# The first head of a hash-attention kernel: copies, sign products and the second head's transposes in another order

## The chip, the cores and the metric

The kernel runs on one core of a Trainium2 chip. The metric is the device time of one execution in microseconds (us), lower is better. TensorE (PE) multiplies matrices, VectorE (DVE), ScalarE (ACT) and GpSimd (POOL) work element by element, and SyncE (SP) issues most DMAs. PEld is PE's loading of weights, which overlaps its multiplications.

## The reference

Four batches of eight heads, 768 positions, head dimension 64. Each position of q and of k gets six sign bits from a projection (64x6); a query sees only keys with the same six bits. A feed-forward stage follows on all heads of a batch side by side.

```python
q_bits = (np.einsum('bhsd,dk->bhsk', q, proj) > 0)
k_bits = (np.einsum('bhsd,dk->bhsk', k, proj) > 0)
mask = q_bucket[:, :, :, None] == k_bucket[:, :, None, :]
scores = np.where(mask, scale * np.matmul(q, k.transpose(0, 1, 3, 2)), -1e9)
attn = softmax(scores)
x = np.matmul(attn, v)          # heads side by side: 512 columns
xk = mu_k * x + (1 - mu_k) * x_prev
xr = mu_r * x + (1 - mu_r) * x_prev
kk = np.maximum(xk @ w_k, 0)
out = sigmoid(xr @ w_r) * (kk * kk @ w_v)
```

## The kernel before

The work goes by pairs of heads: 16 pairs `n`, two heads `j` in each. One head's keys fall into six chunks of 128. A **slot** is one such chunk: two matmuls score all 768 queries against 128 keys (`score`, L451), ScalarE takes the exponential out of PSUM (L458), and two slots later PE multiplies it with the values (`pv`, L478). There are 192 slots. The loop over slots (L750) writes out the order of every engine's queue by hand: in slot G come the score of G, the value product of G-2, pieces of the feed-forward stage of the batch before (from pair 4 on), and what the table `first_block` names for the first slots. Nothing reorders it: an instruction that waits holds up all that stands behind it on its engine. A score tile has two buffers in PSUM, so the score of slot G waits for the exponential of G-2.

The mask is folded into the score. Each operand (`aq`, `ak`) has 70 rows: 64 of q or k, and six rows of +0.5 or -0.5 from the sign bits. A scaled exponential with a large negative bias then sends pairs with different bits to zero. So a score needs three things on each side: transposed q or k in fp32 (`tq`, `tk`), its cast to bf16 in the 64 rows, and the six sign rows.

- `turn` (L311) transposes one side of one head with three matmuls into a PSUM bank, copies the bank to `tq` or `tk`, and casts its two halves of 384 positions into the 64 rows (L336, L337). With `copy=True` ScalarE does the copy (L325) and the second half (L327) and GpSimd the first half (L326). Otherwise VectorE copies (L330 for q, L332 for k), and the casts are done by the engines in `casts`: `pool2` is GpSimd for both, the default is GpSimd and VectorE.
- `bits_direct` (L391) is used for the first pair: one fp32 matmul (two passes) with a projection that lies in `projd` for both halves, and then VectorE makes the sign rows, one instruction for each half of 384 positions (L397). `bits` (L403) does the same for a whole pair and moves the rows by DMA.
- `projd` is filled on VectorE (L695) from `projp`, which is loaded by a DMA on ScalarE's queue behind half of k (L73).
- The PSUM banks A, B, C and D hold one tile each; a new tile waits until the last one was read. Score tiles lie in a pool of their own with two buffers.
- Ahead of the first data, 22 matmuls on constants (L686) keep PE busy.

The order of PE before the loop is: idle matmuls, transposes of q and k of the first head, sign products of both (`bdq`, `bdk`), transposes of q and k of the second head. Then slot 0's score, slot 1's score, the second head's sign product of q, slot 2's score, its sign product of k, and slot 0's value product ahead of slot 3's score. VectorE's order is: copy of q, three copies of the projection, sign rows of q and k, copies of the second head, its sign rows.

Later, GpSimd also casts the values (`values`, L423), and moves the column for the shifted x (`turn_out`, L509), for which VectorE's difference `df` (L521) waits.

## Time and profile before

| what | value |
|---|---|
| three runs | 265.42, 265.53, 266.64 us; median 265.53 |
| profiled execution | 266.43 us, span 264.6 us |
| PE busy | 250.3 us, 95% of the span |
| ACT busy | 216.1 us, 82% |
| DVE busy | 180.0 us, 68% |
| POOL busy | 123.0 us, 46% |
| first transposes on PE | 4.09 us |
| first score on PE | 9.94 us |
| first exponential on ACT | 10.46 us |

The profiled execution is one of its own, outside of the three runs. The span is the time between the first and the last instruction; what lies around it is 1.8 us. The times below count from the span's start. In a timeline row the first number is the start, the second the busy time, "x3" the number of instructions that were merged, and the bracket says how long the engine was idle before and what ended that. In the chain of waits each row is a piece of the one path that leads to the last instruction. Matmuls overlap in the array, so rows of PE can begin before the one above has ended.

### The profile page before, as it was taken

Reading aid. Unit: us, or ns where it says so; the run is one execution under the profiler, and the core shown is the slowest. Engines: PE = TensorE matmul, PEld = TensorE weight load, DVE = VectorE, ACT = ScalarE, POOL = GpSimd, SP = SyncE. Lnnn points to the kernel's source line nnn. Section 1 sums busy time; section 2 is a strip of 40 time slices with the busy share of each in tenths; the row PEclk is TensorE's granted clock in tenths of the full one; section 3 lists DMA queues with packets and bytes.
Section 4 is the critical chain, followed back from the end, with each engine's and each line's share of the span. In section 5 each row is a group of like instructions: output and inputs, shape, how many; then the busy total and the mean of one; then the engine's idle time right before and its main releaser. Section 6 shows DMA issues by size and latency. Waiting matters only on the chain.

```text
span 264.6 us, 6633 instructions
## 1 busy us (share of the span) xinstructions
PE 250.3 (95%) x2441; PEld 151.5 (57%) x2441; DVE 180.0 (68%) x377; ACT 216.1 (82%) x320; POOL 123.0 (46%) x251
## 2 busy tenths in 40 slices
PE   6999999998999999999999999998999999999990
PEld 5566656665565656565665656564656665455450
DVE  2675588769897766759587876778595746776440
ACT  3388879988999998979999998988999988079600
POOL 3669798695766472804574474607492000000000
PEclk9999999999999999999999999999999999999998
DMA  7923695976959291949575483959310002220132
GB/s 217 372 69 54 217 256 92 161 175 119 235 142 185 65 222 34 236 150 247 152 174 109 113 173 88 208 191 237 95 57 8 1 2 83 79 79 0 39 142 73
DMA packets 26488, 35.41 MB, mean 134 GB/s; under 512 B 3064, under 2 KB 22992, under 8 KB 26448
## 3 DMA queue, kind: packets, MB, share of 16 engines
q1 hardware_dynamic: 23936, 31.89, 46.4%
q0 software_dynamic: 2144, 2.62, 6.7%
q8 instruction: 21, 0.34, 0.6%
q10 hardware_dynamic: 368, 0.39, 0.5%
q14 instruction: 19, 0.16, 0.2%
HBM read 30.68 MB, written 6.29 MB: 140 GB/s over the span
## 4 chain that ended last, share of the span: by engine, by line
PE 72%; ACT 9%; DVE 7%; POOL 4%; DMA 2%; issue 2%; SPq 0%; ACTq 0%; DVEq 0%; POOLq 0%
PE sc L451 17%; PE vp L553 15%; PE kp L553 14%; PE oo L478 9%; ACT pt L458 8%; PE rp L553 7%; PE bb L369 3%; PE oo L469 2%; PE ot L503 2%; PE bb L409 1%; DMA vf<-in_v_dram 1%; DMA qk<-in_q_dram 1%; PE bdq L395 1%; DVE ob L490 1%; DVE kr L578 1%
## 5 line engine op out<-in xcount | busy, mean ns | idle before, releaser
L458 ACT ACTIVATE pt<-sc,expb 128x768 bf16<-128x768 f32 x192 | 167.7, 910 | 20.6 <-PE sc L451 18.6
L451 PE MATMUL sc<-aq,ak 70*128 70x384 bf16 x384 | 93.7, 325 | 1.8 <-ACT pt L458 0.7
L478 PEld LDWEIGHTS <-pt 128*128 128x128 bf16 x1152 | 60.5, 97 | 26.5 <-issue 0.2
L478 PE MATMUL oo<-va,pt 128*128 128x65 bf16 x1152 | 66.3, 193 | 0.0
L553 PE MATMUL kp<-xk,wk_sb 128*128 128x384 bf16 x256 | 55.7, 325 | 2.8 <-DVE kr L578 1.1
L553 PE MATMUL vp<-wv_sb,k 128*128 128x512 bf16 (+1 forms) x200 | 51.9, 370 | 0.0
L451 PEld LDWEIGHTS <-ak 70*128 70x128 bf16 x384 | 34.8, 98 | 27.6 <-issue 6.7
L586 DVE TENSOR_TENSOR k<-kr 128x384 bf16<-128x384 bf16 x64 | 27.1, 438 | 6.4 <-ACT kr L576 5.9
L553 PEld LDWEIGHTS <-wk_sb 128*128 128x128 bf16 x256 | 21.7, 97 | 14.3 <-issue 3.8
L353 POOL CAST aq<-tq 64x768 bf16<-64x768 f32 x20 | 16.5, 824 | 26.8 <-PE sc L451 11.7
L553 PE MATMUL rp<-wr_sb,xr 128*128 128x512 bf16 x96 | 28.9, 379 | 0.1
L576 ACT ACTIVATE kr<-kp 128x384 bf16<-128x384 f32 x36 | 18.1, 503 | 8.0 <-PE kp L553 8.0
L553 PEld LDWEIGHTS <-k 128*128 128x128 bf16 x200 | 16.7, 97 | 12.9 <-issue 2.7
L509 POOL COPY xt<-xt 128x127 bf16<-128x127 bf16 x12 | 3.5, 294 | 42.6 <-DVE xt L504 42.5
L439 POOL TENSOR_TENSOR s<-vf 128x192 f32<-128x192 f32 x32 | 22.7, 708 | 0.0
L618 DVE SCALAR_TENSOR_TENSOR os<-th,vp 128x512 f32<-128x512 bf16 (+1 forms) x25 | 16.5, 661 | 7.3 <-PE vp L553 5.4
L489 DVE RECIPROCAL rc<-oo 128x6 f32<-128x6 f32 x32 | 6.1, 191 | 21.9 <-PE oo L478 21.8
L578 DVE TENSOR_SCALAR kr<-kp 128x384 bf16<-128x384 f32 x28 | 15.4, 551 | 7.3 <-PE kp L553 7.1
L504 DVE COPY xt<-ot 128x768 bf16<-128x768 bf16 x16 | 8.9, 556 | 14.8 <-PE ot L503 14.8
L490 DVE TENSOR_TENSOR ob<-oo,rc 128x384 bf16<-128x384 f32 x32 | 17.8, 557 | 1.1
L355 POOL TENSOR_SCALAR ak<-tk 64x768 bf16<-64x768 f32 x20 | 16.6, 832 | 2.8 <-DVE tk L343 1.3
L303 ACT ACTIVATE sq<-blk 128x768 bf16<-128x768 f32 x20 | 17.0, 852 | 0.0
(83 smaller groups left out, 305.5 us busy)
## 6 DMA issues: line engine op xcount, KB each, us to landing
blk<-in_q_dram SPq DMA_DIRECT2D x40, 176.0 KB
blk<-in_k_dram SPq DMA_DIRECT2D x40, 176.0 KB
vf<-in_v_dram SPq DMA_DIRECT2D x16, 384.0 KB
out_dram<-os SPq DMA_DIRECT2D x23, 256.0 KB
qk<-in_q_dram SPq DMA_DIRECT2D x5, 384.0 KB
qk<-in_k_dram SPq DMA_DIRECT2D x5, 384.0 KB
wk_sb<-in_moe_w_k_dram POOLq DMA_DIRECT2D x2, 512.0 KB, 5.5
wv_sb<-in_moe_w_v_dram POOLq DMA_DIRECT2D x2, 512.0 KB, 5.8
```

The source lines that it names most:

```text
L303: nc.scalar.activation(junk.rearrange("p (u d) -> p u d", u=NTOK), blks[n][:, i, :, 0:32], AF.Square, scale=1.5, accum_out=nrm[:, i, n : n ...
L353: eng.tensor_copy(dst, src)
L355: eng.tensor_scalar(out=dst, in0=src, scalar1=ALPHA, scalar2=1.0, op0=ALU.mult, op1=ALU.mult,)
L439: nc.gpsimd.tensor_add(s3, vf[:, 0 : 3 * D], vf[:, 3 * D : 6 * D])
L451: nc.tensor.matmul(sc[:, sp, 0:HALF], au["k", j][:, jc * P : (jc + 1) * P], au["q", j][:, sp * HALF : (sp + 1) * HALF], start=True, stop=True,
L458: nc.scalar.activation(pt.rearrange("p (s q) -> p s q", s=2), sc[:, :, 0:HALF], AF.Exp, bias=expb, scale=SCALE,)
L478: nc.tensor.matmul(oo[:, ic, :], pts[n, j, jc][:, ic * P : (ic + 1) * P], vas[n, j][:, jc, :], start=False, stop=(jc == NC_ - 1 and ic == ...
L490: nc.vector.tensor_tensor(out=obs[n][:, :, j * D : (j + 1) * D], in0=oo[:, :, 0:D], in1=rc.to_broadcast([P, NC_, D]), op=ALU.mult,)
L553: nc.tensor.matmul(box["t"], lhs(), rhs(), start=(i == 0), stop=(i == len(mms) - 1))
L576: nc.scalar.activation(kr, kp, AF.Relu, scale=HALFROOT)
L578: nc.vector.tensor_scalar(out=kr, in0=kp, scalar1=0.0, scalar2=HALFROOT, op0=ALU.max, op1=ALU.mult,)
L586: lambda: nc.vector.tensor_tensor(out=k2, in0=kr, in1=kr, op=ALU.mult),
```

## The change

Five things are done, all in the launch order; the result's arithmetic is the same.

1. Ahead of q's copy VectorE makes the two copies of the projection into `projd`; the third copy (`projp`, needed from the second pair on) comes after k's copy.
2. For the first head, q is copied with `copy=True` (ScalarE twice, GpSimd one cast) and k with `pool2` (VectorE's copy, GpSimd both casts); before, it was the other way round.
3. k's sign product is cut into two pieces, keys 0 to 127 in bank B and 128 to 383 in bank C. VectorE makes k's sign rows in four instructions (128, 256, 128 and 256 positions) instead of two of 384.
4. The second head's transposes move from ahead of slot 0's score to behind it (slot 0 of `first_block`). Idle matmuls: 26 instead of 22 ahead of the data, and eight new ones between k's sign product and slot 0's score, in one buffer of the score pool.
5. At slots 11 and 13 the second half of k's cast for pair 2 goes to VectorE instead of GpSimd.

```diff
-            def bits_direct(n, i, j, which):
+            def bits_direct(n, i, j, which, cuts=(0, HALF)):
 
                 side = "qk"[i]
-                bb = bank(which, [P, HALF], FP32, f"bd{side}{n}_{j}")
-                nc.tensor.matmul(bb, projd, t32s[n, side, j], start=True, stop=True)
+                parts = []
+                for w, lo, hi in zip(which, cuts, cuts[1:]):
+                    bb = bank(w, [P, hi - lo], FP32, f"bd{side}{n}_{j}_{lo}")
+                    nc.tensor.matmul(
+                        bb, projd, t32s[n, side, j][:, lo:hi], start=True, stop=True
+                    )
+                    parts.append((lo, hi, bb))
                 for e in range(2):
-                    nc.vector.tensor_scalar(
-                        out=augs[n % NSET][side, j][D:AUG, e * HALF : (e + 1) * HALF],
-                        in0=bb[D + 32 * e : D + 32 * e + NB, :],
-                        scalar1=0.0, scalar2=0.5, op0=ALU.is_gt, op1=ALU.subtract,
-                    )
+                    for lo, hi, bb in parts:
+                        nc.vector.tensor_scalar(
+                            out=augs[n % NSET][side, j][D:AUG, e * HALF + lo : e * HALF + hi],
+                            in0=bb[D + 32 * e : D + 32 * e + NB, :],
+                            scalar1=0.0, scalar2=0.5, op0=ALU.is_gt, op1=ALU.subtract,
+                        )
...
             idle = bank("A", [P, P], FP32, "idle")
-            for _ in range(22):
+            for _ in range(26):
                 nc.tensor.matmul(idle, epsm, epsm, start=True, stop=True)
             pool2 = (nc.gpsimd, nc.gpsimd)
-            turn(0, 0, 0, "B", pool2)
-            turn(0, 1, 0, "D", copy=True)
-            for dst in (
-                projd[0:D, D : D + NB],
-                projd[D:P, D + 32 : D + 32 + NB],
-                projp[D:P, NB : 2 * NB],
-            ):
+            for dst in (projd[0:D, D : D + NB], projd[D:P, D + 32 : D + 32 + NB]):
                 nc.vector.tensor_copy(dst, projp[0:D, 0:NB])
+            turn(0, 0, 0, "B", copy=True)
+            turn(0, 1, 0, "D", pool2)
+            nc.vector.tensor_copy(projp[D:P, NB : 2 * NB], projp[0:D, 0:NB])
             bits_direct(0, 0, 0, "A")
-            bits_direct(0, 1, 0, "C")
+
+            bits_direct(0, 1, 0, "BC", (0, P, HALF))
+            idle = scp.tile([P, P], FP32, name="idle1", tag="sc")
+            for _ in range(8):
+                nc.tensor.matmul(idle, epsm, epsm, start=True, stop=True)
...
             values(0, 0)
-            turn(0, 0, 1, "B", pool2)
-            turn(0, 1, 1, "D", pool2)
+
+            def turn_second():
+                turn(0, 0, 1, "B", pool2)
+                turn(0, 1, 1, "D", pool2)
+
...
             first_block = {
+                0: turn_second,
...
                 10: lambda: turn(2, 0, 0, "B", pool2),
-                11: lambda: turn(2, 1, 0, "D", pool2),
+                11: lambda: turn(2, 1, 0, "D"),
                 12: lambda: turn(2, 0, 1, "B", pool2),
-                13: lambda: turn(2, 1, 1, "D", pool2),
+                13: lambda: turn(2, 1, 1, "D"),
             }
```

## The prediction, made before the changed kernel ran

> **What bounds the kernel now.** I read the busy shares first, then the chain of waits over the first 14 us, then the timeline of that stretch engine by engine, because every edit but one lies before the fourth score.

> ```profile
> PE 250.3 (95%) x2441; PEld 151.5 (57%) x2441; DVE 180.0 (68%) x377; ACT 216.1 (82%) x320; POOL 123.0 (46%) x251
> ```

> TensorE is busy 95% of the span and its queue is fixed by hand, so an end that moves by some amount at the start moves the end of the kernel by as much, unless a wait further on swallows it. The chain of waits says what the start consists of:

> ```profile
> 4.09 0.89 PE tpq L318 x3
> ...
> 5.65 0.51 DVE projd L695
> ...
> 6.30 1.62 PE bdq L395 x2
> 7.92 1.29 PE bdk L395 x2
> ...
> 9.23 0.56 DVE ak L397
> ...
> 9.82 0.56 DVE ak L397
> ...
> 10.41 0.57 DVE tq L330
> ...
> 11.03 0.91 PE bdq L395 x2
> 11.94 0.33 PE sc L451 x2
> 12.27 0.65 PE bdk L395 x2
> ```

> Read it as: q's transposes, the projection's copy on VectorE, q's and k's sign products, k's sign rows in two halves, then the second head's copy of q (tq, 10.41), its sign product, and only then the third score. The first score ran at 9.94 and is not on this chain: the third score (11.78) is. From there on PE stands in its own queue: no row of PE up to the fourth score (13.10) has a wait, while ScalarE waits for it:

> ```profile
> 12.30 0.90 ACT L458 ACTIVATE pt<-sc,expb 128x768 bf16<-128x768 f32 x1 [0.15 <-PE sc L451]
> ```

> So the number to work out is when the third score issues.

> One later place also counts. Between 24 and 30 us the chain lies on GpSimd, whose casts end in xt, for which VectorE waits; behind that wait stand copies that PE needs at 33.17:

> ```profile
> 30.02 0.56 DVE L521 TENSOR_TENSOR df<-xt 128x768 bf16<-128x768 bf16 x1 [2.64 <-POOL xt L509]
> ...
> 33.17 0.55 PE L318 MATMUL tpk<-ident,qk 128*128 128x128 f32 x3 [0.43 <-DVE tk L332]
> ```

> **The change part by part, against the profiled execution (266.43 us, 264.6 of it span).**

> *Projection ahead of q, q copied by ScalarE.* Before, VectorE copies q (5.01 to 5.57) and then the projection; its second copy takes 0.50 us against 0.15 of the first, and bdq starts at 6.30, 0.14 after it. After, the projection's copies stand first on VectorE. Its DMA landed at 4.80 by the trace's landings, so two copies of 0.15 end near 5.2, at most 5.55 if the second again takes 0.50. ScalarE, idle there, copies q in 0.49 (row L325): 5.01 to 5.50. So bdq starts at 5.50+0.14 = 5.64, 0.66 earlier. ScalarE's second copy of q (0.49, to 6.0) frees bank B, and VectorE's copy of k (from 5.65, 0.55, to 6.20) feeds bdk, which stands behind bdq until 7.05: both hidden, with 0.8 us to spare. GpSimd's casts of k (two of 0.50) now end near 7.3, before a first score at 8.9 or later: hidden. Four more idle matmuls (22 take 2.53, one each 0.107) end near 3.85, before q's transposes at 4.09: nothing.

> *k's sign product in two pieces.* On PE it is the same 384 columns: bdq 5.64, bdk 7.05, free at 8.33. On VectorE, q's two rows start at 5.64+1.62+0.04 = 7.30 and take 1.13, to 8.43. Then four pieces of k (128, 256, 128, 256 columns) instead of two of 384. The trace has no 128-column piece; a copy of 8 columns takes 0.17 (L710) and one of 384 takes 0.56, so a piece lies between these. A straight line gives 0.29 and 0.42, which I take. First piece ends at 8.73, third at 9.46, fourth at 9.89.

> *Eight idle matmuls, then the first score.* They run 8.33 to 9.18 at 0.107 each, where the first piece alone would let the score go at 8.73+0.15 = 8.88: 0.3 us later, and on the path 0.06 (next step).

> *Second head's turns behind the first score.* This adds a wait. tpq of the second head takes bank B, so it waits for the third piece (9.46, so 9.60); the first score holds PE to 9.66. Behind it on PE's queue are tpk, the second score, and everything else. Three transposes issue 0.11 apart and are done 0.49 after the first: 10.15. VectorE copies q from 10.19 (before: 10.41) to 10.75, bdq follows at 10.80, the third score 0.75 later (11.03 to 11.78 in the rows): 11.55. Before: 11.78. **Gain 0.22 us**, a third of what bdq won: pieces, the wait for bank B and the later transposes give the rest back. The second score issues at 10.32 and its exp runs from 10.85 (before 11.26), so ScalarE only waits longer before the third.

> *Key casts of pair 2 half on VectorE.* GpSimd loses two casts of 0.50, so xt comes about 1.1 earlier; df, tq and aq then run early, but the reciprocal behind them (31.36) waits for head sums that PE ends near 31.13, so the rest of that queue comes only 0.19 earlier and PE's wait of 0.43 shrinks by that. VectorE gains two casts of 0.36 to 0.64 (rows L337), the first ahead of the next q copy (23.46, where it had 0.25 idle). That pushes the k copy that the sign products at 25.41 wait for by 0.11 to 0.39, of which they have about 0.1 to spare (it ends at 25.22); of the 0.01 to 0.29 left I take 0.13, nearer the short casts, since GpSimd has fewer left to collide with. Net gain 0.06.

> [...]

> **Sum:** 266.43 − 0.22 − 0.06 = 266.15 for a run like the profiled one. The runs' median is 265.53, 0.90 below it, so the same gain of 0.28 gives 265.25, put down as **265.2 us**.

> **The rivals.** They turn on PE's rate. The same pair of bdq matmuls takes 1.62 at 6.30 and 0.91 at 11.03, three transposes 0.87 at 4.09 and 0.49 at 9.54: until about 9.4, PE ran at half speed, though the granted clock reads 1.00.

> *Full speed comes earlier (faster).* With 26 idle matmuls PE's gap before the transposes shrinks from 0.51 to 0.25 and the one before bdq from 0.69 to 0.25. If that brings full speed before bdq, its 1.62 become about 0.95, and the third score wins 0.65 more; if before the transposes, another 0.3 at most, as the projection lands at 4.80. That is 264.3 to 264.6. Against: the times (265.42, 265.53, 266.64, and 266.43 profiled) fall in two groups 1 us apart, just the size of this step, so the median may hold it already, and then 265.2 stands. Chance 0.17. [...]

> *Full speed comes later (slower).* If PE's waits for VectorE put the change past the first scores, the work from 9.4 to 12 (2.32 us busy in that window) runs at half rate. It takes 2.3 longer, less some 0.6 that PE and ScalarE wait there anyway: 265.2 + 1.7 = 266.9. [...] Chance 0.05.

> *The pieces cost as much as halves.* If a piece takes 0.56 whatever its width, the third ends 0.68 later, and the third score comes 0.46 later than before: 265.9. [...] Chance 0.25. For it: VectorE's rows hardly shrink for few partitions (6 rows cost as much as 128). Against: 8 columns take 0.17. Should they take 0.17 each, PE's 9.66 still binds, so nothing is won.

> **How the numbers follow.** Forecast 0.53 (264.9 to 265.6), earlier full speed 0.17 (264.3 to 264.9), costly pieces 0.25 (265.6 to 266.2), later full speed 0.05. Leaving out the slow case and the ends of the others, the range is 264.5 to 266.2. Half a per cent, about what a measurement of this kernel can tell from no change, is 1.33 us: faster than 264.2 needs the earlier clock and every bound at its best (0.06); slower than 266.86 needs the later clock (0.05); within, 0.89.

> **What would show it.** bdq starting near 5.65 and tq on ScalarE at 5.01; VectorE's first piece near 0.29 us; idle matmuls ending after the first piece; the second head's tpq waiting for VectorE or following the first score at once, near 9.6; the third score near 11.55; the wait of df on xt cut to about 1.5 us and PE's 0.43 at tpk halved. I am wrong if the pair of bdq takes 0.9 rather than 1.6 in one profile and not in the other, if the pieces take over 0.4, or if the third score's shift does not arrive at the end of the span.

## The result, and the profile after

The changed kernel takes 264.48 us (median of 7 runs, 264.12 to 265.05) against 266.11 (7 runs, 265.42 to 267.34) of the kernel before, run beside it: ratio 0.9949, with a 95% interval of 0.9926 to 0.9972. Run again on another occasion it took 264.15 against 265.55, ratio 0.9958 [0.9939, 0.9977]. By these ratios it is faster by about 1.1 to 1.4 us (the medians are 1.63 and 1.40 apart), where 0.28 was forecast; the median of 264.48 lies at the low end of the range, just below its 264.5. The profiled execution took 264.6 us, 262.8 of it span: 1.8 us less than the profiled one of before.

The busy shares of the changed kernel (engine, busy us, share of the span, instructions):

```profile
PE 248.8 (95%) x2455; PEld 151.1 (57%) x2455; DVE 181.3 (69%) x381; ACT 216.4 (82%) x320; POOL 122.1 (46%) x249
```

PE is busy 1.5 us less, although it has 14 instructions more. Work does not vanish that way: some of it ran faster. The chain of waits over the first 14 us (start, us, what) shows which:

```profile
1.19 3.49 DMA projp<-in_proj_dram
...
4.96 0.18 DVE projd L695
...
5.27 0.90 PE bdq L397 x2
...
6.75 0.56 DVE aq L403
...
7.35 0.30 DVE ak L403
...
7.78 0.50 PE sc L457 x2
...
8.38 0.52 PE tpq L318 x3
8.90 0.33 PE tpk L318 x3
9.23 0.33 PE sc L457 x2
9.56 0.91 PE bdq L397 x2
10.46 0.33 PE sc L457 x2
```

Three things are to be seen. The projection's load now stands at the head: its landing, not q's copy, releases the sign products. The two `bdq` matmuls take 0.90 where they took 1.62: PE is at full speed from the start of this chain. And the third score, the last row, is done by 10.79, where before's issued only at 11.78. On ScalarE the third exponential follows it:

```profile
10.83 0.90 ACT L464 ACTIVATE pt<-sc,expb 128x768 bf16<-128x768 f32 x1 [0.33 <-PE sc L457]
```

It starts at 10.83 instead of 12.30, 1.47 earlier. The second place is VectorE around the wait for GpSimd's column (timeline of VectorE, changed kernel):

```profile
27.34 0.56 DVE L527 TENSOR_TENSOR df<-xt 128x768 bf16<-128x768 bf16 x1 [1.43 <-POOL xt L515]
27.81 0.55 DVE L330 COPY tq<-tpq 128x384 f32<-128x384 f32 x1
28.47 0.87 DVE L337 CAST aq<-tq 64x384 bf16<-64x384 f32 x1
29.26 0.18 DVE L495 RECIPROCAL rc<-oo 128x6 f32<-128x6 f32 x1
```

The wait is 1.43 instead of 2.64, and PE's wait of 0.43 at `tpk` is gone from its list of waits. Each slot has one exponential, so their starts tell how far one execution is ahead of the other, slot by slot. By them the changed kernel is 1.47 ahead at slot 21 and 2.44 ahead at slot 27. So 0.97 comes from this place. Later it gives two pieces back, which the waits of PE between 55 and 90 us and of VectorE between 172 and 182 us show:

```profile
PE ot L509 <- DVE ob L496: 0.5, 1, 0.5
```

```profile
DVE os L624 <- DMA out_dram<-os: 1.9, 1, 1.9
```

The lead falls by 0.45 between slots 60 and 68 at the first, and by 0.48 between slots 148 and 156 at the second. In the repeated profile of the same kernel neither is there: it was 2.51 ahead at slot 27 and 2.55 at slot 191. These two belong to the execution, not to the change. At the last exponential it is 1.37 ahead, at the end of the span 1.8; why the tail behind the last exponential is shorter too stays open.

So the profiled pair shows three candidates: a faster beginning that the edits may or may not have caused, above all PE's early full speed, 1.19; the order of the copies, 0.29; the casts, 0.97. The first two are told apart below.

### The profile page after: what moved, and what is told of

It reads as the page before. It is cut to its first block, busy times and chain, and to the rows that moved or that the text cites. A ratio compares the mean times of both kernels' runs of the same rounds, so it can differ in the third digit from the quotient of the medians.

```text
span 262.8 us, 6663 instructions
## 1 busy us (share of the span) xinstructions
PE 248.8 (95%) x2455; PEld 151.1 (57%) x2455; DVE 181.3 (69%) x381; ACT 216.4 (82%) x320; POOL 122.1 (46%) x249
## 4 chain that ended last, share of the span: by engine, by line
PE 72%; ACT 13%; DVE 7%; DMA 4%; issue 2%; ACTq 0%; SPq 0%; DVEq 0%
PE sc L457 17%; PE vp L559 15%; PE kp L559 12%; ACT pt L464 11%; PE oo L484 9%; PE rp L559 7%; PE bb L369 2%; PE bb L415 2%; DMA aq<-sg 2%; PE oo L475 2%; PE ot L509 2%; DMA projp<-in_proj_dram 1%; ACT sq L303 1%; DVE os L624 1%; DVE k L592 1%
```

## The experiments

The theories: **A**, the added idle matmuls bring PE's full speed earlier, and that is the gain; **B**, the moment of full speed follows a phase of each run, and the new order of the copies is the gain; **D**, the casts of edit 5 alone make it. Each expectation says what its theories give; the first two also set the prediction's sum (theory 2) against the reading of the two traces (theory 1). Kernels of one group below were run beside the same runs of before: 265.75 us in the first group (35 runs, 264.57 to 266.18), 265.55 in the second (23 runs) and 265.72 in the third (27 runs). A bracket behind a ratio is its 95% interval. "Copy order" below means edits 1 and 2.

### First group: the casts and the idle matmuls, each alone and left out

**Casts alone** (before, with edit 5 only):

```diff
-                11: lambda: turn(2, 1, 0, "D", pool2),
+                11: lambda: turn(2, 1, 0, "D"),
-                13: lambda: turn(2, 1, 1, "D", pool2),
+                13: lambda: turn(2, 1, 1, "D"),
```

> The kernel before, with only the last edit: the second half of pair 2's key casts on VectorE at slots 11 and 13. Theory 1 (the reading of the two traces): in the changed kernel the exponentials gain 0.96 us more between slots 21 and 27, where ScalarE no longer stops, and this edit makes that gain alone, so about 0.9 us faster. Theory 2 (the prediction's sum): the reciprocal behind the casts waits for PE anyway, so 0.06 us. Theory 3: the 0.96 needs the earlier start too, and this edit alone gives less than 0.3.

Measured: 264.69 us, 0.9965 [0.9947, 0.9982]. So the casts bring 0.93 us (265.75 times 0.0035), most of the whole gain. The trace says how. At the start this kernel has before's instructions, yet at slot 21 its profiled execution is 1.19 ahead of before's: q's data landed earlier (the first transposes run at 3.77 instead of 4.09, so `bdq` starts at 5.97 instead of 6.30), and the rest, 0.86, goes with full speed, which came at 5.09 instead of 9.44. At slot 27 it is 2.16 ahead, which leaves 0.97 for the casts. All ten profiles of kernels with edit 5 gain the same 0.97 between these two slots, early full speed or late. VectorE's timeline in it:

```profile
27.63 0.56 DVE L521 TENSOR_TENSOR df<-xt 128x768 bf16<-128x768 bf16 x1 [1.44 <-POOL xt L509]
...
28.69 0.35 DVE L337 CAST aq<-tq 64x384 bf16<-64x384 f32 x1
28.96 0.18 DVE L489 RECIPROCAL rc<-oo 128x6 f32<-128x6 f32 x1
...
32.90 0.53 DVE L332 TENSOR_SCALAR tk<-tpk 128x384 f32<-128x384 f32 x1
```

The reciprocal starts at 28.96 instead of 31.36: 2.40 earlier, 1.21 more than the 1.19 of the start. The whole queue behind `xt` moved by the 1.20 that the wait lost. On PE three things follow, and the lead of the exponentials prices each. The transposes of q ahead of slot 22's score no longer stand behind VectorE's copy out of their bank (before: copy 30.50 to 31.05, transposes at 31.10), and the lead grows by 0.17. The wait of 0.43 at `tpk` ahead of slot 24's score is gone, and the lead grows by 0.45. The third is the burst of eight sign products of pair 3 ahead of slot 27's score, with the k copy at 32.90, which has to end first. PE's timeline of before, at the burst's first product and at what follows it:

```profile
35.51 0.51 PE L409 MATMUL bb<-tq,projp 128*32 128x384 f32 x1
...
36.65 0.34 PE L469 MATMUL oo<-vs,epsm 128*128 128x390 bf16 x1
```

And the same two rows with the casts alone:

```profile
33.70 0.51 PE L409 MATMUL bb<-tq,projp 128*32 128x384 f32 x1
...
34.48 0.34 PE L469 MATMUL oo<-vs,epsm 128*128 128x390 bf16 x1
```

Before, that k copy ran from 35.29 to 35.82, into the burst, which took 36.65 − 35.51 = 1.14; here it was done at 33.43, and the burst takes 0.78. The lead grows by 0.35. 0.17 + 0.45 + 0.35 = 0.97.

**No casts** (the changed kernel without edit 5; the diff above, reversed):

> The changed kernel without its last edit: both halves of pair 2's key casts on GpSimd again. Theory 1: about 0.9 us slower than the changed kernel, some 0.5 to 0.8 us faster than before. Theory 2: 0.06 us from the changed kernel. In both the first 21 slots run as in the changed kernel.

Measured: 265.86 us, 1.0019 [0.9997, 1.0041]. All the edits at the start together bring no gain without the casts, where theory 1 expected 0.5 to 0.8. Its profile is 1.43 ahead of before's at slot 3, most of which is early full speed again (at 4.50). Part of the lead is lost in PE's waits between 20 and 36 us (us in total, times, longest):

```profile
PE tpk L318 <- DVE tk L332: 0.9, 1, 0.9
```

The wait at `tpk` is 0.93 in the timeline, not 0.43. VectorE's and GpSimd's timelines of this kernel say why:

```profile
29.73 0.87 DVE L337 CAST aq<-tq 64x384 bf16<-64x384 f32 x1
```

```profile
29.69 0.50 POOL L336 CAST aq<-tq 64x384 bf16<-64x384 f32 x1 [1.12 <-DVE tq L330]
```

And the same pair in before:

```profile
31.08 0.35 DVE L337 CAST aq<-tq 64x384 bf16<-64x384 f32 x1
```

```profile
31.11 0.69 POOL L336 CAST aq<-tq 64x384 bf16<-64x384 f32 x1 [1.12 <-DVE tq L330]
```

In these two pairs the cast that starts first takes the shorter of its two times and the other the longer: VectorE first, 0.35 and 0.69; GpSimd first, 0.87 and 0.50. VectorE, 0.04 behind GpSimd, takes 0.87 − 0.35 = 0.52 more, about GpSimd's whole 0.50; GpSimd, 0.03 behind VectorE, takes 0.69 − 0.50 = 0.19 more. What makes them take longer side by side was not shown. The order flips with who copied q for pair 0. With the new copy order VectorE's `aq` cast waits for two semaphores and its `ak` cast for one; in before it is the other way round. In the changed kernel's trace the second wait is an instruction of its own (0.02 at 28.40), and the cast starts 0.66 after the start of its copy (27.81 to 28.47), in before 0.58 (30.50 to 31.08). So it comes behind GpSimd's: `aq` takes 0.87 in all ten profiles with the new copy order, and 0.35 to 0.36 in the four without. That the semaphore is the reason fits all of these, but it was not varied by itself.

The collision does not cost its whole 0.50, however. The `ak` cast behind it, with one semaphore less, takes 0.35 instead of 0.64. So VectorE catches up, and its next k copy is done at 34.55, before PE comes to the burst of sign products. PE's timeline of no casts shows the short burst:

```profile
34.59 0.51 PE L415 MATMUL bb<-tq,projp 128*32 128x384 f32 x1
...
35.38 0.34 PE L475 MATMUL oo<-vs,epsm 128*128 128x390 bf16 x1
```

That is 0.79 instead of 1.14. By the exponentials the lead falls from 1.42 at slot 21 to 0.92 at slot 24 and is back at 1.27 at slot 27: 0.15 lost. So the traces leave about 0.14 of the start's 0.29, and why the runs show no gain at all is not explained by them. In the changed kernel the casts bring VectorE's whole queue forward by 1.2, and PE has no wait at `tpk` in spite of the 0.87.

**26 idle matmuls alone** (before) and **22 in the changed kernel**:

```diff
-            for _ in range(22):
+            for _ in range(26):
```

> The kernel before, with 26 idle matmuls ahead of the data instead of 22, nothing else. Theory A (the idle matmuls bring PE's full speed earlier): full speed comes before the first sign products in the profile, the third score some 0.7 to 1.2 us earlier, and the time 0.5 to 1 us under before. Theory B (the moment of full speed follows from the run's own phase, not from four matmuls): the time within 0.2 us of before, and the moment anywhere between 4 and 9.5 us.

> The changed kernel with 22 idle matmuls ahead of the data instead of 26, all else as changed. Theory A: PE stops for 0.5 us before q's transposes as it did before, full speed comes later in most runs, and 0.5 to 1 us of the gain goes. Theory B: within 0.2 us of the changed kernel.

Measured: 26 alone 265.07 us, 0.9988 [0.9973, 1.0004]; the changed kernel with 22 264.99, 0.9975 [0.9958, 0.9992]. The first is no difference that can be told from none; the second lies above the changed kernel's 0.9949 and 0.9958, with intervals that overlap. Both profiles show full speed early, with 26 at 5.47 and with 22 at 4.44: theory A's count of matmuls does not decide it. In the profile with 22 the projection could be copied only from 5.13 (changed kernel: 4.78) and VectorE's second copy of it took 0.42, so `bdq` started at 5.88 and the third score at 10.91, 0.61 later than the changed kernel's. Whether that is common in this kernel, or the four idle matmuls make full speed come late in fewer executions, stays open.

### Second group: which of the start's edits help

**The changed kernel again** (no edit), **casts and copy order** (before with edits 1, 2 and 5; k's product whole, turns ahead, 22 idle matmuls), **casts and idle matmuls** (before with edit 5, 26 idle matmuls, and six between k's transposes and q's sign product), and **one piece** (the changed kernel with k's product whole):

```diff
-            turn(0, 0, 0, "B", pool2)
-            turn(0, 1, 0, "D", copy=True)
-            for dst in (
...
+            for dst in (projd[0:D, D : D + NB], projd[D:P, D + 32 : D + 32 + NB]):
                 nc.vector.tensor_copy(dst, projp[0:D, 0:NB])
+            turn(0, 0, 0, "B", copy=True)
+            turn(0, 1, 0, "D", pool2)
...
```

```diff
+            for _ in range(6):
+                nc.tensor.matmul(idle, epsm, epsm, start=True, stop=True)
```

```diff
-            bits_direct(0, 1, 0, "BC", (0, P, HALF))
+            bits_direct(0, 1, 0, "C")
```

> The changed kernel once more, beside the three that follow on the same chip. Theory A (the time of full speed, which a run's phase decides, makes the two groups of the kernel before, and the changed kernel has no late group): all its runs within about 1 us of each other, 264.1 to 265.1, ratio near 0.995. Theory D (the casts alone make the gain): the same time as the kernel before with the casts moved, 264.7, within 0.2.

> The kernel before with the casts moved and with the new order of copies (projection first, q by ScalarE, k by VectorE); k's sign product whole, the second head's turns ahead of the first score, 22 idle matmuls and no more. By the prediction's sum the copies start q's sign product 0.66 us earlier and nothing gives it back, so 0.4 to 0.66 us under casts alone: about 264.1. By theory A alone, whose idle matmuls it lacks, it still has a late group and its runs spread over more than 1.5 us.

> The kernel before with the casts moved, 26 idle matmuls ahead of the data and six more between k's transposes and q's sign product; the copies, the products and the scores in the old order. Theory A: no late group, runs within 1 us of each other, median about 264.2, as good as the whole change or better. Theory B (order of the copies makes the gain of the start): as casts alone, 264.7, with runs of 265.3 to 265.7 among them.

> The changed kernel with k's sign product whole again, in bank C: two rows of VectorE instead of four, and the second head's transposes wait for no piece. The prediction's sum: two halves of 0.56 end 0.3 us before four pieces of 0.29 and 0.42; the first score goes 0.27 later, the third 0.2 earlier, so up to 0.2 us faster than the changed kernel. If instead the early first score is what counts, 0.2 to 0.3 slower.

Measured: the changed kernel 264.15 us, 0.9958 [0.9939, 0.9977]; casts and copy order 263.63, 0.9935 [0.9912, 0.9959]; casts and idle matmuls 264.42, 0.9965 [0.9947, 0.9984]; one piece 263.53, 0.9927 [0.9902, 0.9953].

Filling PE's gap adds nothing to the casts (0.9965 both times), against A; the copy order adds 0.3% to them, with intervals that still overlap. Nor did the pieces help: with k whole the median is lower, not higher, the intervals overlapping. One piece also had the latest full speed of the four profiles, at 9.46 (its `bdq` took 1.62), and still a lower median over its runs: one profile's clock is no property of a kernel.

### Third group: the best version, the load, the copies alone, no eight idle matmuls

**Whole and ahead** (casts and copy order, with 26 idle matmuls), and the same with **the projection loaded on GpSimd's queue**:

```diff
-    nc.scalar.dma_start(out=projp[0:D, 0:NB], in_=proj)
+    nc.gpsimd.dma_start(out=projp[0:D, 0:NB], in_=proj)
```

> The kernel before with the casts moved, the new order of copies and 26 idle matmuls ahead of the data; k's sign product whole, the second head's turns ahead of the first score, no idle matmuls behind it. It is the whole change without the pieces, the later turns and the eight idle matmuls. If those three cost on the path (0.4 us in the traces so far: the second head's copy of q starts 2.8 after q's sign product with them, 2.37 without), it is 0.3 to 0.6 us faster than the changed kernel, ratio 0.993. If the early first score is worth something, it is slower than the changed kernel by 0.2 or more.

> As the run before it, with the projection loaded on GpSimd's queue instead of ScalarE's, where half of k stands ahead of it. In the changed kernel VectorE waits for the projection until 4.7 to 5.2, and q's sign product starts 0.14 after its copies. If it lands before 4.4, the copies are done before ScalarE's copy of q and the product starts about 5.15 at the latest with full speed: up to 0.15 us faster, more in runs like the one where it landed at 5.17. If a load by GpSimd's queue lands later than 4.8, it is slower by as much.

Measured: whole and ahead **263.43 us, 0.9930 [0.9907, 0.9953]**, the lowest median of all, below both kernels. It has the copy order, the casts and the 26 idle matmuls, without pieces, late turns and the eight idle matmuls. Its third score on PE:

```profile
5.29 0.95 PE L395 MATMUL bdq<-tq,projd 128*128 128x384 f32 x2
...
9.97 0.49 PE L451 MATMUL sc<-aq,ak 70*128 70x384 bf16 x2
```

That is 0.33 earlier than the changed kernel's 10.30, from the same start of `bdq` within 0.02. The clock did not make this gain: the changed kernel is at full speed throughout, this one only from 5.39, so its `bdq` takes 0.95 instead of 0.88. From the end of `bdq` to the second head's copy of q pass 2.37 (casts and copy order 2.37, casts alone 2.38), against 2.79 in the changed kernel and 2.80 in its repeat: pieces, the wait for bank B and the late turns cost 0.42 on the path. The same row of casts and copy order, whose instructions differ only by the four idle matmuls, shows the size of the clock:

```profile
5.29 1.65 PE L395 MATMUL bdq<-tq,projd 128*128 128x384 f32 x2
```

0.95 and 1.65 for one pair of matmuls at one time; that execution's full speed came at 7.10. Yet the medians of the two kernels, 263.43 and 263.63, have overlapping intervals.

With the load on GpSimd's queue the time is 266.81 us, 1.0051 [1.0030, 1.0072], slower than before. GpSimd issues it at 1.49 and VectorE can copy from 7.92, where ScalarE's queue had it landed at 4.7. PE's timeline:

```profile
8.41 1.15 PE L395 MATMUL bdq<-tq,projd 128*128 128x384 f32 x2 [3.05 <-DVE projd L689]
9.36 1.48 PE L395 MATMUL bdk<-tk,projd 128*128 128x384 f32 x2
10.64 0.84 PE L318 MATMUL tpq<-ident,qk 128*128 128x128 f32 x3
```

PE stands for 3.05, and the clock that it had at 5.48 is lost again from about 8.9 to 12.3: `bdk` takes 1.48, three transposes 0.84. So half speed at the first scores, which the slower rival feared, does come in this run, after the gap of 3.05. But the run does not price that rival: most of the 3.38 over whole and ahead is the late load itself, with VectorE's copies starting 3.24 later (7.92 against 4.68), as the expectation said of a later landing.

**Copies only** (before with edits 1 and 2), and the changed kernel **without the eight idle matmuls**:

```diff
-            idle = scp.tile([P, P], FP32, name="idle1", tag="sc")
-            for _ in range(8):
-                nc.tensor.matmul(idle, epsm, epsm, start=True, stop=True)
```

> The kernel before with the new order of copies and nothing else: the casts of pair 2 stay on GpSimd. If the two gains add, it is 0.9 us slower than the same kernel with the casts moved (263.6), near 264.6. If the start's gain is lost again at pair 3, where PE waits for VectorE (0.9 us in the changed kernel without the casts), it is no faster than before by more than 0.4.

> The changed kernel without the eight idle matmuls between k's sign product and the first score. Where full speed comes early they end before the first piece, so it is the same as the changed kernel within 0.2 us. Where it comes late they delayed the first score by 0.3 and the third by 0.06: nothing to gain. If they are what keeps full speed on, PE's gap of some 1.1 us brings half speed back in some runs, which would then be 1 us or more slower.

Measured: copies only 264.95 us, 0.9986 [0.9967, 1.0005]; without the eight 264.28, 0.9955 [0.9939, 0.9970], like the changed kernel. PE's waits of copies only, between 20 and 36 us:

```profile
PE tpk L318 <- DVE tk L332: 1.0, 1, 1.0
```

Here too the casts collide, and PE's wait at `tpk` is 0.96 instead of 0.43; here too the burst gives most of it back, and by the exponentials the lead falls from 1.52 at slot 21 to 1.35 at slot 27, 0.17. The intervals leave open whether copies alone gain anything.

### The terms against the times

From the traces: copy order 0.62 (third score 9.97 against 10.59 of casts alone, both at full speed), in the changed kernel 0.29 (10.30); casts 0.97; the collision −0.15 to −0.17 where the casts stay on GpSimd and the copies have the new order. The gain in the runs is (1 − ratio) times the time of before.

| kernel | terms, us | sum | gain in the runs, us [interval] |
|---|---|---|---|
| casts alone | 0.97 | 0.97 | 0.93 [0.48, 1.41] |
| casts and idle matmuls | 0.97 | 0.97 | 0.93 [0.42, 1.41] |
| copies only | 0.62 − 0.17 | 0.45 | 0.37 [−0.13, 0.88] |
| no casts | 0.29 − 0.15 | 0.14 | −0.50 [−1.09, 0.08] |
| casts and copy order | 0.62 + 0.97 | 1.59 | 1.73 [1.09, 2.34] |
| whole and ahead | 0.62 + 0.97 | 1.59 | 1.86 [1.25, 2.47] |
| changed kernel | 0.29 + 0.97 | 1.26 | 1.36 [0.75, 1.97] |
| changed kernel again | 0.29 + 0.97 | 1.26 | 1.12 [0.61, 1.62] |
| without the eight | 0.29 + 0.97 | 1.26 | 1.20 [0.80, 1.62] |
| 26 idle matmuls alone | 0 | 0 | 0.32 [−0.11, 0.72] |
| changed kernel with 22 | 0.29 + 0.97 | 1.26 | 0.66 [0.21, 1.12] |

No term for the clock is in the sums, and nine of eleven intervals hold them. The two that don't are no casts and the kernel with 22 idle matmuls, the two open points above; both are slower than their sums. The intervals are about 1 us wide, so this bears out the casts' term, but it can't tell terms of a few tenths from none. The kernel with one piece isn't listed, since no run prices late turns without pieces by themselves.

## Why the prediction was wrong in size

**The casts' term, 0.06 forecast, 0.97 measured: this step failed.** The wait of `df` on `xt` was forecast at 1.5 and came out at 1.43. But the prediction let the queue behind it stop at "the reciprocal behind them (31.36) waits for head sums that PE ends near 31.13". PE's timeline of before, over that stretch, says otherwise:

```profile
29.19 0.35 PE L478 MATMUL oo<-va,pt 128*128 128x65 bf16 x6
...
30.06 0.33 PE L469 MATMUL oo<-vs,epsm 128*128 128x390 bf16 x1
30.23 0.34 PE L478 MATMUL oo<-va,pt 128*128 128x65 bf16 x6
...
30.78 0.35 PE L478 MATMUL oo<-va,pt 128*128 128x65 bf16 x6
```

The product at 30.78, ended at 31.13, belongs to the next head: the row of `vs` at 30.06 opens that head's bank. The reciprocal's own sums were done at 29.19 + 0.35 = 29.54. It stood at 31.36 in its queue, not in a wait; its row has no bracket. So the whole queue moved by 1.2, not 0.19. The price of VectorE's two new casts, 0.13 of the 0.19, did not show: in casts alone they took 0.35 and 0.66, and its lead of 1.19 is the same at slots 3 and 21. The upper end of the range, 266.2, puts the casts at a cost of 0.3, a term that no run shows: the longest cast of VectorE's beside one of GpSimd's took 0.87 instead of 0.35, and edit 5 still gained 0.97 in all ten profiles that have it.

**Copy order: right.** `bdq` was to start 0.66 earlier; against casts alone, whose start has before's instructions (5.97), it starts 0.66 to 0.68 earlier (5.29 to 5.31) in casts and copy order, whole and ahead, and copies only. (In one piece, where the projection came late, it starts at 5.91.) Two thirds were to be given back by pieces, the wait for bank B and the late turns, leaving 0.22 at the third score: 0.29 was left, and the 0.42 given back showed in the traces. The first piece took 0.30 (0.29 taken), so the rival of costly pieces is out. (Its third score, 0.46 later than before, should be 0.39 by the prediction's own steps, since the first score holds PE for 0.06 of it in any case; the rounded 265.9 is the same.) What it took as fixed was the landing of the projection, which now heads the chain: VectorE's copies begin at 4.78 here, but at 5.17 with one piece and 6.09 without the eight idle matmuls, kernels that differ behind that point only, and at 5.13 with 22. Why it varies stays open.

**Earlier full speed: it came, but the runs do not show it as the cause.** The prediction's own sign of being wrong is there: the pair of `bdq` took 0.9 in one profile and 1.6 in the other. Together with q's data, which landed earlier, full speed at 4.15 instead of 9.44 is worth 1.19 in this pair of profiles, and the rival's 264.3 to 264.6 holds the median. But its condition, the added idle matmuls, brought no gain that can be told from none in the runs that varied it: 26 alone 0.9988 [0.9973, 1.0004], and nothing on top of the casts. The prediction's own remark, that the median may hold the full speed already, fits: before alone varies from 264.57 to 266.18. So the rival named the right number for a reason that the runs do not bear out, and that the forecast range ends next to the median is luck, since the term that made most of the gain was put at 0.06.

**A step left out.** That the new copy order turns round who casts first in pair 3 was not foreseen. Where the casts stay on GpSimd it lengthens PE's wait at `tpk` by 0.5 us, of which 0.35 comes back at the burst.

## What to carry to other kernels

Before you let an instruction hold up a queue, find in the trace the row that it really waits for: a row without a bracket only stood in line, and what moves ahead of it moves it too. Test the edits of a bundle alone and left out: here one small edit far from the others made most of the gain, and two others gave about half of a third one's gain back in the traces. When a wait grows, follow the lead past it before you book the loss: a later, cheaper step may give most of it back. Before comparing two profiles, look at what the same matmuls take in their first microseconds, and take the difference that an earlier or later full speed makes out.

## What the runs showed of the hardware

**Transposes ran at both speeds.** In before three of them take 0.87 ahead of full speed (at 4.09) and 0.49 after it (at 9.54).

**The granted clock read 1.00 where PE was slow.** In before it reads 1.00 up to 9.44, ahead of the first clock record, and the profile's page shows 9 in the first slices of PEclk in before and after alike, while the same pair of `bdq` takes 1.62 and 0.88. The durations tell the speed there, the clock row doesn't.

**The sign rows' time went by columns, not by rows.** VectorE's piece of 6 rows took 0.30 for 128 columns and 0.56 for 384, all four pieces 1.28; a copy of 128 rows and 384 columns takes 0.56 too.
